# A fused retention and PReLU MLP kernel: the last two token blocks go as a pair through all eight units

## Chip, cores and metric

The kernel runs on one core of a Trainium2 chip. The metric is the device time of one execution in microseconds (us); lower is better. The engines are named as the profile names them: PE (TensorE), PEld (its weight loads), DVE (VectorE), ACT (ScalarE), POOL (GpSimd) and SP (SyncE, which issues the DMAs here).

## What is computed

```python
# retention: q, k, v are (B=8, H=8, S=576, D=64)
scores = (1 / np.sqrt(D)) * np.matmul(q, k.transpose(0, 1, 3, 2))
gamma = 1.0 - 2.0 ** (-5.0 - np.arange(H))
rel = pos[:, None] - pos[None, :]
Dmat = np.where(rel >= 0, gamma[:, None, None] ** rel[None], 0.0)
attn = np.matmul(scores * Dmat, v)
# MLP on the same tokens
x = attn.transpose(0, 2, 1, 3).reshape(4608, 512)
h = x @ w_in                                   # (4608, 2048)
g = np.maximum(h, 0) + alpha * np.minimum(h, 0)
out = g @ w_out                                # (4608, 512)
```

All of it is fp32. [...]each operand of a product is split into three pieces (a scaled high part, a low part and a difference), and each product is three matmuls.

## The kernel before, in words

**Tiling.** The 4608 tokens are 18 blocks of 256 (`kb`). The hidden width of 2048 is eight units of 256 (`u`). The work of one block on one unit is a *cell*: a first product (x pieces times w_in pieces, functions `unit` and `unit_two`), the PReLU on ACT and DVE, the split of its result into three pieces in a g tile (`split_g`: two ACT and two POOL operations), and a second product (`second`, g pieces times w_out pieces, summed in the four PSUM banks `pso`). A *visit* is one block going through several units; `order` (line 964) lists the visits. `evacuate` (L1243) takes a visit's sum out of PSUM with the help of DVE, and stores it, either as the result or, where more units are to follow, in the DRAM buffer `ok`. A later visit of the block reads it back into the tile `op`.

**Stages.** SBUF holds the split weights of four units (`wsl`, 4 x 4 tiles). So the first half of the kernel takes blocks 0 to 16 through units 0 to 3, while the attention for later blocks runs in between (`joint`, called at the cells that `todo` lists, the last at cell 56). Block 17 is the *turn*: it goes through all eight units in one visit, and behind it the weights of units 4 to 7 take the place of those of units 0 to 3. The second half takes blocks 0 to 16 through units 4 to 7.

**Singles and pairs.** `unit` (L1132) works on one block: its matmuls have 256 columns (L1151), 12 for each half of the unit, 24 for a cell. `unit_two` (L1171) works on two blocks at once: 24 matmuls for two cells, of 512 columns (L1181), with the results in `psh` for one half and in `psa` for the other. Before the change, the first half and the turn are singles, blocks 0 to 15 of the second half go in eight pairs, and block 16's second half is a single at the very end. The second product (L1232) has 512 columns in both forms.

**x pieces.** `split_x` (L1011) splits a block's x. For a single, the pieces lie in one of the two `lx` tiles (`one_room`). For a pair, `two_rooms` gives the tiles: those of unit 3's weights (`wsl[3]`) and the two `lx` tiles in turn. A block's x is kept in DRAM (`xk`) between its halves. In a pair's split DVE makes the low piece (L1057) and POOL the difference (L1061). Where two columns of pieces lie side by side, one operation takes both (512 elements); where not, each takes 256. Singles from visit `LATE_X` on use a PSUM bank of `psa` for an intermediate, which spares POOL an operation.

**Weights.** In the first half, `convert` brings the weights from the inputs' form into fp32, one quarter unit at a time, and stores those of units 4 to 7 in DRAM (`wk`); it uses the tiles `op` and `wa`. `split_w` (L750) makes three pieces of one quarter. With `raw` it reads the quarter from `wk` by DMA, and, before the change, then takes a form of its own: two ACT operations (one into `psa`) and two DVE operations that read `psa` (L765 to L774). Without `raw` it takes one ACT, one POOL (L775) and one DVE operation (L777). Unit 4's pieces go into the tiles that attention used (`planes`, L1427), and the others into `wsl[0]` to `wsl[2]`.

**What sets the order.** The code doesn't issue instructions as it is read. `do` records operations with engine, cost and dependencies, and `plan` (L226) orders them: it works out due times from the end backwards, and then fills each engine's queue forwards, the operation with the earliest due time first. PE may go at most 150 recorded operations ahead of its order in the program (`AHEAD_PE`). Big DMAs are issued no more than 30 us before they are due (`HOLD`). Operations marked `lock` (all of POOL's tensor operations and those of DVE that read two SBUF operands) are held in one order across POOL and DVE:

```python
for op in best[1]:
    ins = op.fn()
    if op.lock:
        if port and port[0] != op.eng:
            tc.add_manual_dep(ins.ins, port[1].ins.name, ..., reason="port")
        port = op.eng, ins
```

In the pair stage, `pump` (L1516) says how many second products are recorded after each half of a first product: `PUMP0` has five for the first pair and `PUMP` eight for each later one (L339), so five second products are carried from each pair into the next.

Of the kernel before, what the change touches and what calls it, by code (L numbers as in the profile page):

```python
# [17 lines left out]
ALU = mybir.AluOpType  # L18
# [3 lines left out]
def kernel(  # L22
# [10 lines left out]
    nc = tc.nc  # L33
    B, H, S, D = q.shape
    NTOK, DM = out.shape
# [3 lines left out]
    NPAIR = H // 2  # L39
# [3 lines left out]
    NCC = DM // P  # L43
    NFC = DFF // P
    NU = NFC // 2
    TB = 2 * P
    NKB = NTOK // TB
    NS = NU // 2
# [8 lines left out]
    ONE = 1.0 + 2.0 ** -12  # L57
    BELOW = 1.0 - 2.0 ** -13
# [22 lines left out]
    def piece(x):  # L81
        return x.bitcast(PIECE)
# [255 lines left out]
    LAG, HOLD_X = 2, 100.0  # L338
# [411 lines left out]
    def split_w(at, raw=None, planes=None):  # L750
        u, i = divmod(at, 4)
        if raw:
            key = (raw, "w", 0)
            dma(lambda: words_of(raw)[:, 0:DM], lambda: w32[at], P * DM * 4, [(w32m[at], 0)], [key])
        else:
            key = plain[at]
        if planes is None:
            g = Gen(wsl[u if u < NS else u - NS - 1, i])
            planes = [(g, l) for l in range(3)]
        w = w_at[u, i] = planes  # L760
        h, l, d = (lambda n=n: piece(words_of(w[n][0])[:, w[n][1] * DM:(w[n][1] + 1) * DM])
                   for n in range(3))
        hf = lambda: words_of(w[0][0])[:, w[0][1] * DM:(w[0][1] + 1) * DM]
        full = lambda: words_of(key[0])[:, key[2]:key[2] + DM]
        do("ACT", 0.64, lambda: nc.scalar.mul(h(), full(), BELOW), [key], [w[0]])  # L765
        if raw:
            hp = Gen(psa[at % 2])
            do("ACT", 0.6, lambda: nc.scalar.mul(piece(hp.get()), full(), BELOW), [key], [(hp, 0)])
            do("DVE", 0.69, lambda: nc.vector.tensor_tensor(
                out=l(), in0=full(), in1=hp.get(), op=ALU.subtract), [key, (hp, 0)], [w[1]])  # L770
            do("DVE", 0.69, lambda: nc.vector.scalar_tensor_tensor(
                out=d(), in0=hp.get(), scalar=ONE, in1=full(), op0=ALU.mult,
                op1=ALU.subtract), [key, (hp, 0)], [w[2]])
            return  # L774
        do("POOL", 1.29, lambda: nc.gpsimd.tensor_tensor(  # L775
            out=l(), in0=full(), in1=hf(), op=ALU.subtract), [key, w[0]], [w[1]], lock=True)
        do("DVE", 0.7, lambda: nc.vector.scalar_tensor_tensor(  # L777
            out=d(), in0=hf(), scalar=ONE, in1=full(), op0=ALU.mult,
            op1=ALU.subtract), [key, w[0]], [w[2]], lock=True)
# [181 lines left out]
            dma(to, lambda h2=h2: su.get()[half(h2)], (S - C) * D * 4, keys, [(vn, "s", h2)])  # L961


    order = [(kb, (0, 1, 2, 3)) for kb in range(NKB - 1)]
    order += [(NKB - 1, range(NU))]
    order += [(kb, (4, 5, 6, 7)) for kb in range(NKB - 1)]
    visits, cells, seen = [], [], {kb: 0 for kb in range(NKB)}
    for n, (kb, us) in enumerate(order):
        vis = {"kb": kb, "n": n, "has": seen[kb] > 0, "us": us}
# [28 lines left out]
        return {(l, cc): (g, (l * NCC + cc) * TB) for l in range(3) for cc in range(NCC)}, TB  # L998

    def two_rooms(n):  # L1000
        if n % 2:
            gg = [Gen(x) for x in lxs]
            return {(l, cc): (gg[cc // 2], (l * 2 + cc % 2) * DM)
                    for l in range(3) for cc in range(NCC)}, DM
        gg = [Gen(wsl[NS - 1, i]) for i in range(4)]
        at = {(2, cc): (gg[cc], 2 * DM) for cc in range(NCC)}
        at.update({(l, cc): (gg[l * 2 + cc // 2], cc % 2 * DM)
                   for l in range(2) for cc in range(NCC)})
        return at, DM
# [250 lines left out]
            P * DM * 4, [(o, 0)], [(okm[kb], m)])  # L1260


    LATE_X = next(v["n"] for v in visits if 4 in v["us"]) - 3
    spare = Gen(lxs[1])
    raws = iter([((spare, 0), kTs[1]), ((spare, 1024), qTs[1]), ((spare, 2048), was)] +
                4 * [((wsl[0, i], 0), None) for i in range(4)])
# [137 lines left out]
    assert sum(map(len, todo.values())) == len(pairs) - 2 * NPAIR  # L1404


    turn = cells.index(next(c for c in cells if c["u"] == NS)) - NS
    late = {turn - 8 + 2 * i: [16 + i] for i in range(4)}
    for i in range(3):
        for n in range(4):  # L1410
            late.setdefault(turn + 1 + i + n // 2 * LAG, []).append(20 + 4 * i + n)
    raw_rooms = [Gen(None) for _ in range(2)]
    ahead = {10 + 3 * i: 1 for i in range(16)}
    nraw = [0]

    def raw_room():
        n = nraw[0] % 3
        nraw[0] += 1
        if n == 2:
            return Gen(xs[3])  # L1420
        g = Gen(None)
        was = raw_rooms[n] if raw_rooms[n].ops else vnm[n]
        g.before, g.tile = list(was.ops), vns[n]
        raw_rooms[n] = g
        return g

    def planes():  # L1427
        for x in (kxs, qxs, kns[0], kns[1], kTs[0], kTs[1], qTs[0], qTs[1]):
            yield Gen(x), 0
        g = Gen(ats)  # L1430
        yield g, 0
        yield g, 1
        for x in (sus, was):
            yield Gen(x), 0

    def start_x(vis):
        kb = vis["kb"]
        if "from" not in vis and (kb not in xb or NPAIR * (ready_kb[kb] + 1) in done):
            fetch_x(vis)

    pend = []
    turned_to = next(v["n"] for v in visits if 4 in v["us"])
    two = [(visits[n], visits[n + 1]) for n in range(turned_to + 1, len(visits) - 1, 2)]
    for i, (va, vb) in enumerate(two):
        va["two"], vb["two"] = (i, 0), (i, 1)
    visits[-1]["two"] = len(two), 0
    homes_two = {}

    def next_x(vis):
        start_x(vis)  # L1450
        if "from" in vis and "x" not in vis:
            if "two" not in vis:
                split_x(vis)
            else:
                i, side = vis["two"]
                if not side:
                    homes_two[i] = two_rooms(i)
                split_x(vis, homes_two[i], side)

    def at_cell(cell):  # L1460
        n, vis = cell["n"], cell["vis"]
        next_x(vis)
        for _ in range(ahead.get(n, 0)):
            convert((op_, 0), was, None)
        for at in late.get(n, ()):
            if at == 16:
                planes_of.append(planes())
            split_w(at, raw_room(), [next(planes_of[0]) for _ in range(3)] if at < 20 else None)
        unit(cell)
        pend.append(cell)  # L1470
        if len(pend) > LAG:
            second(pend.pop(0))
        split_g(cell)
        for x in todo.get(n, ()):
            joint_(x)

    planes_of = []
    of = {}
    for cell in cells:
        of.setdefault(cell["vis"]["n"], []).append(cell)  # L1480
    for cell in cells[8:]:
        vis = cell["vis"]
        if vis["n"] > turned_to:
            break
        at_cell(cell)
        nxt = vis["n"] + 1
        if vis["n"] < turned_to:
            if cell["last"] or vis["n"] > 3:
                start_x(visits[nxt])
                if cell["last"]:  # L1490
                    next_x(visits[nxt])
        elif cell["u"] in (NS + 1, NS + 2):
            next_x(visits[nxt + cell["u"] - NS - 1])

    ga_rooms = [xs[2], xs[3], xs[4]]
    ga_kept = [raw_rooms[n] for n in range(2)]
    nga = [0]

    def ga_room():
        n = nga[0] % 5  # L1500
        nga[0] += 1
        if n < 3:
            return Gen(ga_rooms[n])
        g = Gen(None)
        g.before, g.tile = list(ga_kept[n - 3].ops), vns[n - 3]
        ga_kept[n - 3] = g
        return g

    queue = list(pend)
# [1 line left out]
    def ahead_g(k=2):  # L1511
        for c in queue[:k]:
            if "ga" in c and "g" not in c:
                split_g(c)

    def pump(k):  # L1516
        for _ in range(k):
            if queue and "ga" in queue[0]:
                ahead_g(1)
                second(queue.pop(0))  # L1520
                ahead_g()

    for i, (va, vb) in enumerate(two):
        ca, cb = of[va["n"]], of[vb["n"]]
        queue += ca + cb
        for nu, (a, b) in enumerate(zip(ca, cb)):
            ga = ga_room()
            for f in range(2):
                unit_two(va, vb, a["u"], ga, f)
                if f:  # L1530
                    for side, c in enumerate((a, b)):
                        c["ga"] = ga, lambda ga=ga, side=side: words_of(ga)[
                            :, 0:2 * DM].rearrange("p (f s t) -> p f s t", f=2, s=2)[:, :, side]
                    ahead_g()
                pump((PUMP if i else PUMP0)[nu][f])
            nxt = va["n"] + 2 + (nu - 1)
            if nu in (1, 2) and nxt < len(visits):
                next_x(visits[nxt])
    for cell in of[visits[-1]["n"]]:
        unit(cell)  # L1540
        queue.append(cell)
        pump(3)
        ahead_g()
    pump(len(queue))
    best = plan()

# [40 lines left out]
```

## Time and profile before

| what | value |
|---|---|
| median of 3 runs | 931.44 us (930.61 to 931.87) |
| the profiled execution's own time | 930.41 us |
| its span, first to last instruction | 928.7 us |
| cells as singles / in pairs | 80 / 64 |
| DMA issues that matter here: `xk<-x`, `x<-xk` | 18, 17 of 512 KB |
| `ok<-o`, `op<-ok` | 34 of 256 KB, 17 of 512 KB |
| `vn<-wk`, `x<-wk` (weights of units 4 to 7) | 11 and 5 of 256 KB |

The page of the profile gives each engine's busy time, then groups of instructions by line, engine and operation as "out<-in", with their count, busy time and mean. The chain of work that ended last is followed back from the last instruction: at each step to what released it. A view by stages gives each engine's busy time in chosen stretches, the instructions begun there, PE's granted clock, the DMA engines' share, and GB/s. L1151 is line 1151 of the kernel.

### The profile page before, as it was taken

Reading aid. Unit: us, or ns where it says so; the run is one execution under the profiler, and the core shown is the slowest. Engines: PE = TensorE matmul, PEld = TensorE weight load, DVE = VectorE, ACT = ScalarE, POOL = GpSimd, SP = SyncE. Lnnn points to the kernel's source line nnn. Section 1 sums busy time; section 2 is a strip of 40 time slices with the busy share of each in tenths; the row PEclk is TensorE's granted clock in tenths of the full one; section 3 lists DMA queues with packets and bytes.
Section 4 is the critical chain, followed back from the end, with each engine's and each line's share of the span. In section 5 each row is a group of like instructions: output and inputs, shape, how many; then the busy total and the mean of one; then the engine's idle time right before and its main releaser. Section 6 shows DMA issues by size and latency. Waiting matters only on the chain.

```text
span 928.7 us, 20968 instructions
## 1 busy us (share of the span) xinstructions
PE 918.4 (99%) x8101; PEld 779.4 (84%) x8101; DVE 532.5 (57%) x1070; ACT 552.6 (60%) x1178; POOL 579.3 (62%) x491
## 2 busy tenths in 40 slices
PE   8999999999999999999999999999999999999998
PEld 7676798988888898988999988888888888888887
DVE  7677666667666667766755764443454444434333
ACT  4566557566666667666876885554546363635342
POOL 5676867558765677655666465837465655647363
PEclk9999999999999999999999999999999999999999
DMA  9997587798887859864444421121212222221112
GB/s 231 241 233 144 127 203 151 176 206 175 195 199 193 193 138 221 191 150 130 148 137 147 126 80 68 47 91 46 91 54 82 68 86 95 70 68 46 46 46 68
DMA packets 235524, 120.93 MB, mean 130 GB/s; under 512 B 203408, under 2 KB 203424, under 8 KB 235424
## 3 DMA queue, kind: packets, MB, share of 16 engines
q1 hardware_dynamic: 235424, 119.59, 50.9%
q8 instruction: 64, 1.05, 0.5%
q14 instruction: 36, 0.29, 0.1%
HBM read 74.19 MB, written 31.98 MB: 114 GB/s over the span
## 4 chain that ended last, share of the span: by engine, by line
PE 90%; DMA 3%; DVE 2%; POOL 2%; SPq 1%; issue 1%; ACT 1%; POOLq 0%; DVEq 0%; ACTq 0%
PE pso L1232 39%; PE psh L1151 22%; PE psh L1181 9%; PE psa L1181 9%; PE psh L851 3%; PE psa L913 2%; PE psh L1082 2%; PE pso L1113 1%; SPq L208 1%; POOL w L775 1%; DMA kn<-in_k_dram 1%; DMA w<-in_moe_w_in_dram 1%; PE psh L903 1%; PE psa L910 1%; DMA lx<-in_moe_w_in_dram 0%
## 5 line engine op out<-in xcount | busy, mean ns | idle before, releaser
L1232 PE MATMUL pso<-w,g 128*128 128x512 f32 x1416 | 347.1, 392 | 0.0
L1232 PEld LDWEIGHTS pso<-w,g 128*128 128x128 f32 x1416 | 259.6, 188 | 50.7
L1151 PEld LDWEIGHTS psh<-lx,w 128*128 128x128 f32 x1608 | 202.4, 191 | 8.4 <-ACT x L870 1.1
L1151 PE MATMUL psh<-lx,w 128*128 128x256 f32 x1608 | 208.5, 284 | 0.7 <-ACT x L870 0.5
L1211 POOL TENSOR_TENSOR g<-g 128x512 fp32r<-128x512 f32 x136 | 176.0, 1294 | 24.2 <-DVE w L1057 4.1
L1208 POOL TENSOR_TENSOR g<-ga,g 128x512 fp32r<-128x512 f32 x72 | 93.2, 1294 | 122.9 <-ACT g L1204 107.9
L1159 DVE SCALAR_TENSOR_TENSOR ga<-psh,ga 128x256 f32<-128x256 f32 x144 | 60.6, 421 | 70.6 <-ACT ga L1158 68.9
L1158 ACT COPY ga<-psh 128x256 f32<-128x256 f32 x144 | 53.5, 372 | 69.5 <-PE psh L1151 60.8
L1208 POOL TENSOR_TENSOR g<-x,g 128x512 fp32r<-128x512 f32 x40 | 51.7, 1295 | 63.5 <-ACT g L1204 61.0
L1165 DVE SCALAR_TENSOR_TENSOR ga<-psh,malpha,ga 128x256 f32<-128x256 f32 x144 | 68.6, 477 | 22.4 <-ACT psh L1162 21.4
L1061 POOL TENSOR_TENSOR lx<-lx 128x512 fp32r<-128x512 f32 x48 | 61.9, 1296 | 20.1 <-DVE lx L1057 13.1
L1162 ACT ACTIVATE psh<-ga 128x256 f32<-128x256 f32 x144 | 55.7, 387 | 30.4 <-DVE ga L1159 30.2
L1204 ACT ACTIVATE g<-ga 128x512 fp32r<-128x512 f32 x72 | 45.4, 631 | 22.3 <-DVE ga L1165 15.0
L1208 POOL TENSOR_TENSOR g<-vn,g 128x512 fp32r<-128x512 f32 x24 | 31.1, 1294 | 41.6 <-ACT g L1204 38.4
L931 DVE SCALAR_TENSOR_TENSOR at<-psa,pf,mask 64x512 f32<-64x512 f32 x48 | 36.0, 750 | 25.8 <-PE psa L910 24.9
L1206 ACT ACTIVATE g<-ga 128x512 fp32r<-128x512 f32 x72 | 44.7, 621 | 0.0
L1250 DVE TENSOR_TENSOR op<-pso,op 128x512 f32<-128x512 f32 x34 | 23.3, 686 | 36.8 <-PE pso L1232 36.7
L1204 ACT ACTIVATE g<-x 128x512 fp32r<-128x512 f32 x40 | 25.1, 630 | 32.1 <-PE pso L1232 17.1
L1188 DVE SCALAR_TENSOR_TENSOR x<-psh,x 128x512 f32<-128x512 f32 x20 | 13.8, 690 | 45.0 <-PE psh L1181 45.0
L851 PEld LDWEIGHTS psh<-at,vn 128*64 128x64 f32 x864 | 27.7, 137 | 10.8 <-issue 6.0
L1057 POOL TENSOR_TENSOR lx<-x,lx 128x512 fp32r<-128x512 f32 x24 | 31.1, 1295 | 8.7 <-ACT lx L1054 5.4
L1181 PE MATMUL psh<-lx,w 128*128 128x512 f32 x144 | 34.7, 389 | 0.0
(292 smaller groups left out, 1695.9 us busy)
## 6 DMA issues: line engine op xcount, KB each, us to landing
xk<-x SPq DMA_DIRECT2D x18, 512.0 KB, 4.1
out_dram<-o SPq DMA_DIRECT2D x36, 256.0 KB, 2.0
ok<-o SPq DMA_DIRECT2D x34, 256.0 KB, 3.2
x<-xk SPq DMA_DIRECT2D x17, 512.0 KB, 5.7
op<-ok SPq DMA_DIRECT2D x17, 512.0 KB, 4.0
qx<-in_q_dram SPq DMA_DIRECT2D x96, 72.0 KB, 3.4
kx<-in_k_dram SPq DMA_DIRECT2D x96, 72.0 KB, 3.1
kn<-in_k_dram SPq DMA_DIRECT2D x48, 144.0 KB, 3.7
```

What stands on the lines that cost most here:

```text
L851: nc.tensor.matmul(pv[i].get()[half(h2), (j - js[0]) * C:(j - js[0] + 1) * C], vns[n % 2][:, h2, j], mt.get()[:, h2, j], start=True, stop= ...
L1061: lambda l=l, d=d, h=view(0, c): nc.gpsimd.tensor_tensor(out=piece(d()), in0=h(), in1=l(), op=ALU.subtract),
L1151: nc.tensor.matmul(at(b), w[:, c0:c0 + P], xp(l, cc), start=(n == 0 and cc == 0), stop=(n > 0 and cc == NCC - 1), skip_group_check=True)
L1158: do("ACT", 0.36, lambda g=g, at=at: nc.scalar.copy(g(), at(1)), [(ph, 1)], [(ga, f)])
L1159: do("DVE", 0.42, lambda g=g, at=at: nc.vector.scalar_tensor_tensor(out=g(), in0=at(0), scalar=ONE, in1=g(), op0=ALU.mult, op1=ALU.subtrac ...
L1162: do("ACT", 0.39, lambda g=g, at=at: nc.scalar.activation(at(1), g(), ACTF.Relu, scale=-1.0), [(ga, f)], [(ph, 1)])
L1165: do("DVE", 0.48, lambda g=g, at=at, fc=fc: nc.vector.scalar_tensor_tensor(out=g(), in0=at(1), scalar=malpha[:, fc:fc + 1], in1=g(), op0=A ...
L1181: nc.tensor.matmul(p.get(), w[:, c0:c0 + P], piece(words_of(g)[:, o:o + DM]), start=(l != 1 and cc == 0), stop=(l > 0 and cc == NCC - 1))
L1204: do("ACT", 0.64, lambda: nc.scalar.mul(piece(to.get()[:, 2]), whole(), BELOW), both, [(to, 2)])
L1208: do("POOL", 1.29, lambda: nc.gpsimd.tensor_tensor(out=piece(to.get()[:, 1]), in0=whole(), in1=to.get()[:, 2], op=ALU.subtract), both + [( ...
L1211: do("POOL", 1.29, lambda: nc.gpsimd.tensor_tensor(out=piece(to.get()[:, 2]), in0=to.get()[:, 0], in1=to.get()[:, 1], op=ALU.subtract), [( ...
L1232: nc.tensor.matmul(a[2 * m + b].get(), piece(g.get()[:, l, f, m * P:(m + 1) * P]), w_piece(u, 2 + f, l), start=(cell["first"] and f == 0 a ...
```

## The change

The visits are ordered anew. Blocks 0 to 15 go through units 0 to 3 as singles. Then blocks 16 and 17 go as a pair through units 3, 0, 1, 2 and as a pair through units 4 to 7, on the same x pieces. Then blocks 0 to 15 go in eight pairs through units 4 to 7. Every cell from the turn on is in a pair: 64 cells as singles and 80 in pairs. Block 17's half sum is now stored and read back like that of every other block.

The x pieces of the first pair, and of every second pair after it, lie in the tiles that attention used (`planes`); the pairs between use `wsl[3]` as before. Unit 4's weight pieces go into the two `lx` tiles. The weights of unit 5 + u are split in two steps, by the new `split_later`: those of its first product after unit u's first product in the first pair, and those of its second product after unit u's second product for block 17. The raw quarters are read into `x3`, `x4` and the two `ga` tiles. The form of `split_w` with two DVE operations on `psa` is gone: all quarters take the one with an ACT, a POOL and a DVE operation, the last two under the lock. `LATE_X` is 15 in place of 14.

```diff
@@ split_w @@
         do("ACT", 0.64, lambda: nc.scalar.mul(h(), full(), BELOW), [key], [w[0]])
-        if raw:
-            hp = Gen(psa[at % 2])
-            do("ACT", 0.6, lambda: nc.scalar.mul(piece(hp.get()), full(), BELOW), [key], [(hp, 0)])
-            do("DVE", 0.69, lambda: nc.vector.tensor_tensor(
-                out=l(), in0=full(), in1=hp.get(), op=ALU.subtract), [key, (hp, 0)], [w[1]])
-            do("DVE", 0.69, lambda: nc.vector.scalar_tensor_tensor(
-                out=d(), in0=hp.get(), scalar=ONE, in1=full(), op0=ALU.mult,
-                op1=ALU.subtract), [key, (hp, 0)], [w[2]])
-            return
         do("POOL", 1.29, lambda: nc.gpsimd.tensor_tensor(
@@ order of the visits @@
-    order = [(kb, (0, 1, 2, 3)) for kb in range(NKB - 1)]
-    order += [(NKB - 1, range(NU))]
-    order += [(kb, (4, 5, 6, 7)) for kb in range(NKB - 1)]
+    order = [(kb, (0, 1, 2, 3)) for kb in range(NKB - 2)]
+    order += [(kb, (3, 0, 1, 2)) for kb in (NKB - 2, NKB - 1)]
+    order += [(kb, (4, 5, 6, 7)) for kb in (NKB - 2, NKB - 1, *range(NKB - 2))]
@@ two_rooms @@
-        if n % 2:
-            gg = [Gen(x) for x in lxs]
-            return {(l, cc): (gg[cc // 2], (l * 2 + cc % 2) * DM)
-                    for l in range(3) for cc in range(NCC)}, DM
+        if n % 2 or n == 0:
+            rooms_of = ((g, i * DM) for g, i in planes())
+            return {(l, cc): next(rooms_of) for l in range(3) for cc in range(NCC)}, DM
@@
-    LATE_X = next(v["n"] for v in visits if 4 in v["us"]) - 3
+    LATE_X = NKB - 3
@@ when weights are split @@
-    turn = cells.index(next(c for c in cells if c["u"] == NS)) - NS
-    late = {turn - 8 + 2 * i: [16 + i] for i in range(4)}
-    for i in range(3):
-        for n in range(4):
-            late.setdefault(turn + 1 + i + n // 2 * LAG, []).append(20 + 4 * i + n)
+    turn = cells.index(of[NKB - 2][0])
+    late = {turn - 4: [16], turn - 3: [17]}
...
@@ start_x @@
-        if "from" not in vis and (kb not in xb or NPAIR * (ready_kb[kb] + 1) in done):
+        if vis.get("two", (0,))[0] == 1:
+            at, step, side = visits[vis["n"] - 2]["x"]
+            vis["x"] = at, step, side
+        elif "from" not in vis and (kb not in xb or NPAIR * (ready_kb[kb] + 1) in done):
             fetch_x(vis)
@@ pairs @@
-    turned_to = next(v["n"] for v in visits if 4 in v["us"])
-    two = [(visits[n], visits[n + 1]) for n in range(turned_to + 1, len(visits) - 1, 2)]
+    singles = NKB - 2
+    two = [(visits[n], visits[n + 1]) for n in range(singles, len(visits), 2)]
     for i, (va, vb) in enumerate(two):
         va["two"], vb["two"] = (i, 0), (i, 1)
-    visits[-1]["two"] = len(two), 0
...
+    def split_first(at):
+        if at % 2 == 0:
+            planes_of[:] = [Gen(lxs[at // 2 % 2])]
+        split_w(at, Gen(xs[3 + at % 2] if at < 18 else gas[at % 2]), [(planes_of[0], at % 2 * 3 + l) for l in range(3)])
...
@@ the cells of the singles @@
-        elif cell["u"] in (NS + 1, NS + 2):
-            next_x(visits[nxt + cell["u"] - NS - 1])
+        if nxt == singles:
+            if cell["u"] < 2:
+                next_x(visits[nxt + cell["u"]])
...
@@ pump @@
-                second(queue.pop(0))
+                c = queue.pop(0)
+                second(c)
+                if c["vis"]["n"] == singles + 1 and c["u"] < NS - 1:
+                    split_later(c["u"], 1)
                 ahead_g()
+
+    def split_later(u, half_of):
+        for n in range(2):
+            at = (NS + 1 + u) * 4 + 2 * half_of + n
+            split_w(at, Gen(gas[at % 2]))
@@ the pairs @@
                 pump((PUMP if i else PUMP0)[nu][f])
+            if i == 0:
+                if a["u"] < NS - 1:
+                    split_later(a["u"], 0)
+                else:
+                    split_first(18)
+                    split_first(19)
...
-    for cell in of[visits[-1]["n"]]:
-        unit(cell)
-        queue.append(cell)
-        pump(3)
-        ahead_g()
     pump(len(queue))
```

The rest of the diff is room keeping: `raw_room` and its counters go, and the pairs' `ga` tiles begin with `vn0` and `vn1` in place of `x2`.

More of the change, by code (lines that the diff above doesn't have):

```diff
@@ L1404 @@
     assert sum(map(len, todo.values())) == len(pairs) - 2 * NPAIR
-    turn = cells.index(next(c for c in cells if c["u"] == NS)) - NS
-    late = {turn - 8 + 2 * i: [16 + i] for i in range(4)}
-    for i in range(3):
-        for n in range(4):
-            late.setdefault(turn + 1 + i + n // 2 * LAG, []).append(20 + 4 * i + n)
+    of = {}
+    for cell in cells:
+        of.setdefault(cell["vis"]["n"], []).append(cell)
+    turn = cells.index(of[NKB - 2][0])
+    late = {turn - 4: [16], turn - 3: [17]}
     raw_rooms = [Gen(None) for _ in range(2)]
     ahead = {10 + 3 * i: 1 for i in range(16)}
[L1414 to L1425, printed above, removed]
     def planes():
@@ L1465, in at_cell @@
         for at in late.get(n, ()):
-            if at == 16:
-                planes_of.append(planes())
-            split_w(at, raw_room(), [next(planes_of[0]) for _ in range(3)] if at < 20 else None)
+            split_first(at)
         unit(cell)
@@ L1477 @@
     planes_of = []
-    of = {}
-    for cell in cells:
-        of.setdefault(cell["vis"]["n"], []).append(cell)
+    def split_first(at):
+        if at % 2 == 0:
+            planes_of[:] = [Gen(lxs[at // 2 % 2])]
+        split_w(at, Gen(xs[3 + at % 2] if at < 18 else gas[at % 2]), [(planes_of[0], at % 2 * 3 + l) for l in range(3)])
     for cell in cells[8:]:
         vis = cell["vis"]
-        if vis["n"] > turned_to:
+        if vis["n"] == singles:
             break
@@ L1486 @@
         nxt = vis["n"] + 1
[L1487 to L1491, printed above, removed]
-        elif cell["u"] in (NS + 1, NS + 2):
-            next_x(visits[nxt + cell["u"] - NS - 1])
+        if nxt == singles:
+            if cell["u"] < 2:
+                next_x(visits[nxt + cell["u"]])
+        elif cell["last"] or vis["n"] > 3:
+            start_x(visits[nxt])
+            if cell["last"]:
+                next_x(visits[nxt])
     ga_rooms = [xs[2], xs[3], xs[4]]
-    ga_kept = [raw_rooms[n] for n in range(2)]
-    nga = [0]
+    nga = [3]
     def ga_room():
@@ L1504, in ga_room @@
         g = Gen(None)
-        g.before, g.tile = list(ga_kept[n - 3].ops), vns[n - 3]
-        ga_kept[n - 3] = g
+        g.before, g.tile = list(raw_rooms[n - 3].ops or vnm[n - 3].ops), vns[n - 3]
+        raw_rooms[n - 3] = g
         return g
```

## The prediction, made before the changed kernel ran

> **What bounds the kernel now.** First the head and the busy totals of the page.
>
> ```profile
> span 928.7 us, 20968 instructions
> PE 918.4 (99%) x8101; PEld 779.4 (84%) x8101; DVE 532.5 (57%) x1070; ACT 552.6 (60%) x1178; POOL 579.3 (62%) x491
> ```
>
> PE is never idle for long; the other engines have a third of the time free. So the question is what PE does in each stage. The chain of work that ended last, asked for the stretches around the turn (start, length, piece):
>
> ```profile
> 497.73 2.87 PE psh L1151 x24
> 500.61 2.75 PE pso L1232 x12
> 503.35 2.87 PE psh L1151 x24
> ...
> 572.84 2.72 PE psh L1181 x12
> 575.56 2.72 PE psa L1181 x12
> 578.28 5.44 PE pso L1232 x24
> ...
> ```
>
> From about 440 us the chain is PE alone, back to back. A cell of a single block costs 2.87 + 2.75 = 5.62 us. Two cells of a pair cost 2.72 + 2.72 for the first product and 5.44 for the second: 10.88, or 5.44 a cell. Over whole pairs (L1181 on psh begins a pair at 653.24 and the next at 696.84) it is 43.60 for eight cells, 5.45 each. The end of the same chain:
>
> ```profile
> 912.59 2.87 PE psh L1151 x24
> 915.46 9.56 PE pso L1232 x42
> 925.02 0.05 issue
> 925.07 0.69 DVE o L1255
> ```
>
> The last single cell's chain through ACT, DVE and POOL is fully covered: 42 matmuls were held back for it. From 925.07 on there are the last evacuation and its store, 3.6 us to the span's end.
>
> Then the reserve of the others, by stage (columns: PE, PEld, DVE, ACT, POOL busy):
>
> ```profile
> 200.00:250.00 50.00, 49.88 (x587) 43.83 (x586) 34.17 (x77) 35.53 (x84) 39.72 (x32) 1.00 0.92 199
> 440.00:481.00 41.00, 41.00 (x291) 37.27 (x286) 26.31 (x53) 33.45 (x76) 28.94 (x23) 1.00 0.41 131
> 548.00:584.00 36.00, 36.00 (x160) 29.82 (x159) 16.87 (x26) 23.16 (x44) 21.46 (x18) 1.00 0.13 45
> 610.00:653.60 43.60, 43.60 (x194) 35.95 (x193) 18.74 (x28) 22.63 (x41) 25.59 (x21) 1.00 0.23 73
> ```
>
> POOL and the DVE operations marked lock are put in one order by the code (lines 1547 to 1555), so their times add. I call the sum the **port**. In 200 to 250 it was 39.72 + 4.6 (three weight conversions at 0.42 + 0.42 + 0.69 us of DVE) = 44.3 of 50 us, 89%, and PE still ran 49.88. In a steady pair it is 25.59 + 2.77 = 28.4 of 43.6.
>
> **What the Trainium skill says.** "TensorE: Matmul & The Clock Gate", section "Wait — 56ns, not 53.3ns?": a warm matmul starts every N/2.4 GHz plus 2.5 ns. The trace has 2.72/12 = 226.7 ns for 512 columns and 2.87/24 = 119.6 for 256: the difference, 107.1 ns for 256 columns, agrees with 2.4 GHz, but the fixed part is 12.5 ns here. The measurement decides; this fixed part is what a pair saves. "SBUF — State Buffer", section "Who interferes with whom": a DVE instruction with two SBUF inputs blocks against a GpSimd one that reads SBUF, one with a single SBUF input does not. The code's lock follows that: the old weight split reads its second operand from PSUM and takes no lock, the new one does. The trace shows the waits of the ordering (below), not the hardware's. "Perfetto Trace Analysis", section "Identifying the Most-Contended Engine": matmul busy time is a poor measure; so I use start-to-start times, not the 99%.
>
> **The change part by part.**
>
> *Pairs for singles.* 16 cells (eight of block 17, four of block 16's first half, four of its second) leave the single form for eight pair cells. First product: 8 x (2 x 2.87 - 5.44) = 2.40 us less. Second: 16 x (2.75 - 2.72) = 0.48 less. Sum -2.88, all of it on PE, which sets the end.
>
> *One more trip through DRAM.* Block 17 was summed over eight units in PSUM; now its half sum is stored and read back: 36 evacuated visits for 35, two more stores of 256 KB, one more read of 512 KB (3.2 and 4.0 us to landing). A pair's surplus over 16 x 2.72 is 43.60 - 43.52 = 0.08 for its two evacuations, so one more is 0.04; with rounding +0.1 on PE. The copy on ACT (0.59) and the DVE operations (0.69 each) lie under PE. Against it, block 16's x is read back and split once less (one DMA and about eight POOL and DVE operations); block 17 had no second split. SP issues at 0.3 to 0.6 us each with DMA at 0.13 to 0.23 of its time there: nothing.
>
> *The tail.* The last five second products now follow the last pair's first product with no other work between. From the end of such a first product to its last piece the steady trace has about 5.7 us (psa unit ends near 615.1, POOL L1211 ends at 620.8). Two second products (5.44) can be held back for it, three if g's three buffers allow. Between 0 and 0.5; I take +0.2. After that POOL needs 2.59 a cell against PE's 2.72. Evacuation and store stay 3.6.
>
> *Attention must be finished for both blocks at the turn.* Block 17's x was needed at 480.9, now both are, but what they wait for, the last attention copy (L870), starts at 441.1. That leaves 40 us, in which the pieces go into attention's tiles. One of these (wa) is also the conversions' buffer, so the last conversion, which ended at about 492, must come some 20 us earlier; the planner's due times pull it. Port in that stage: 28.94 + about 5 of DVE locks, + 4 x (0.74 + 0.42) x 2 for two narrow splits, + 2 x 1.97 for two weights, less a late split (2.6) and a conversion or two: about 42 of 41 us on paper if nothing moved, but work of 10 us can go into 400 to 440, where POOL is below 0.7 busy. Nothing taken, up to 2 us if it doesn't fit.
>
> *The weights of units 4 to 7.* Sixteen splits change form: ACT 0.63 + 0.59 and DVE 2 x 0.68, unlocked, become ACT 0.63, POOL 1.28 and DVE 0.69, both in the port: +1.97 each, +31.5 us of port. The moved DMA reads (16 of 256 KB, about 3 us to landing) stay on SP, later than before. Two lie before the turn; two, and the six first-product ones, in the first pair (but units 7's two only as it ends); six second-product ones in the second pair.
>
> The second pair is the tightest place. The narrow x split there, by form (count, busy, mean ns, idle before and releaser):
>
> ```profile
> L1057 DVE TENSOR_TENSOR w<-x,w 128x256 fp32r<-128x256 f32 x28 | 10.9, 421 | 22.3 <-POOL g L1208 14.4 <-POOL g L1211 4.6 <-POOL w L1061 3.2
> L1061 POOL TENSOR_TENSOR w<-w,w 128x256 fp32r<-128x256 f32 x28 | 20.1, 743 | 11.6 <-DVE w L1057 11.6
> ```
>
> g: 8 x 2.59 = 20.7. Weights: 6 x 1.97 = 11.8, and 3.9 left over from unit 7. x for the third pair: 8 x (0.42 + 0.74) = 9.3. Handing over: POOL to DVE 0.03, DVE to POOL about 0.11 (637.50 to 637.53, 638.22 to 638.30, 636.05 to 636.20), 16 turns x 0.14 = 2.2. Sum 47.9, against 43.6 of PE. But three g can be made ahead in the first pair (-7.8): 40.1, 92%. The first pair then has 8 x 2.59 + 6 x 1.97 + 0.8 = 33.3 of 35.4, 94%. It fits, above the 89% that was seen to cost nothing. I take +0.1; the bounds are 0 and 6.
>
> DVE waits at these locks with the chains of L1188 and L1193 queued behind, and those release the next g; POOL has g itself behind it. That is the danger.
>
> **Sum.** -2.88 + 0.1 + 0.2 + 0.1 = -2.5. The profiled execution took 930.41 (span 928.68 and 1.73 around it): 927.9. The median 931.44 lies 1.0 above that execution, so **928.9**.
>
> **The rivals.** Faster or slower than 931.44 by over 0.2% (1.9 us) is about what can be told from no change: 929.6 and 933.3.
>
> *Gain eaten.* The spare 5% of the port isn't usable: the x pieces can't begin before unit 3's last second product frees its tiles, some 11 us into the second pair, and from there to its end x 9.3 + weights 11.8 + four g 10.4 + turns 2.0 = 33.5 stand against 32.7. With 0.8 over, and as much in the first pair: 930.5, no difference. For it: L1057 stood 22.3 us waiting on POOL even in quiet pairs. Against it: PE may put second products later, and a pair later the port has 12 us free.
>
> *Slower: the port in the second pair.* A locked DVE operation stands behind an unlocked one of 0.69 to 0.75, on average half of it, 0.36, while POOL waits its turn: L1061's 11.6 us over 28 shows 0.41 each already. With the handover 0.5 a turn; 14 turns x 0.5 = 7 on 42.0 makes 49 against 43.6: +5.4 us of PE idle, 934.3. It decides from 4.4 us of overflow on.
>
> *It doesn't do what it says.* The planner keeps singles' speed, say by splitting the pair's x late at the turn, so that PE waits 2 to 3 us once: 931.5.
>
> **How the numbers follow.** Forecast 928.9 (928.2 to 929.6): 0.58. Gain eaten 0.20 and the late turn 0.08: together 0.28 within 0.2%. Slower 0.14. The range reaches from 928.0, the full 2.9 with the scatter of 0.5 that the runs show, to 932.5, which leaves out the slower case and little else.
>
> **What would show it.** PE busy about 916; no L1151 after the turn; the first pair begins near 481, and each later one takes 43.6. Waits of PE for g (POOL L1211) or x (L1061) between 490 and 565 would be the port; a gap near 481 the late turn; a gap before the last second products the tail. The forecast is wrong if PE's idle time after 440 is over 1 us besides the end, or if a pair form's cell isn't 5.45 in the new pairs.

## The result and the profile after

The changed kernel took 929.44 us (median of 22 runs, 927.5 to 933.23) against 931.87 for the kernel before in the same runs: ratio 0.9977, 95% interval 0.9969 to 0.9985. A second set gave 928.82 against 931.96, ratio 0.9967 (0.9957 to 0.9976). So it is faster by 2 to 3 us; 928.9 was forecast, 2.5 us below.

The profiled execution took 931.02 (span 929.3), in the slower half of the 22. It has to be read by stages and not by its span. The head of its page:

```profile
span 929.3 us, 20609 instructions
PE 915.8 (99%) x7909; PEld 770.7 (83%) x7909; DVE 518.9 (56%) x1040; ACT 542.0 (58%) x1164; POOL 601.2 (65%) x525
```

There are 192 matmuls fewer and as many weight loads fewer; PE is busy 2.6 us less, POOL 21.9 us more. In the changed kernel L1151 is now L1141, L1181 is L1171, L1232 is L1222. L1198 and L1201 are POOL's two operations for a g tile, L766 and L768 POOL's and DVE's for a weight quarter, L1051 and L1047 those for an x split. The chain of work that ended last, from the last singles on (start, length, piece):

```profile
471.71 2.87 PE psh L1141 x24
474.59 2.29 PE pso L1222 x10
476.88 2.87 PE psh L1141 x24
479.75 4.11 PE pso L1222 x18
483.86 2.72 PE psh L1171 x12
486.58 2.72 PE pso L1222 x12
489.30 2.72 PE psa L1171 x12
...
513.78 2.73 PE pso L1222 x12
516.60 0.64 ACT g L1194
517.31 1.31 POOL g L1198
518.64 0.70 DVE w L768
519.48 1.30 POOL g L1198
520.77 0.77 issue
521.58 1.30 POOL g L1201
522.92 2.12 PE pso L1222 x8
525.04 2.72 PE psa L1171 x12
```

The turn comes at 483.7, and no 256-column matmul follows it. The x for the two blocks was there in time. In the second pair the chain leaves PE for once: a second product waits for its g, which POOL could begin only after a weight split of DVE (L768) that came first in the common order. This is the port (POOL and the locked DVE operations taken together), and what it costs is small: from start to start, two matmuls there take 0.24 and 0.11 us more than their 0.227. It is the only place after the turn where one takes over 0.1 us more.

The end of the chain:

```profile
901.05 2.72 PE psa L1171 x12
903.77 21.77 PE pso L1222 x96
925.54 0.04 issue
925.58 0.69 DVE o L1245
```

Eight second products were held back for the tail, where I had thought of two or three, and they run without a gap.

The stages of the changed kernel (columns: PE, PEld, DVE, ACT, POOL busy), the second pair last:

```profile
440.00:481.00 41.00, 40.96 (x289) 36.76 (x288) 22.74 (x50) 30.99 (x76) 32.26 (x29) 1.00 0.32 108
481.00:517.00 36.00, 36.00 (x160) 29.82 (x159) 17.08 (x26) 20.83 (x39) 20.69 (x17) 1.00 0.40 127
517.00:560.50 43.50, 43.42 (x192) 35.62 (x191) 22.41 (x38) 29.12 (x59) 32.98 (x29) 1.00 0.31 98
```

I cut the profiled executions, two of each kernel, at the first matmul of the first split cell, at the turn (the 57th such cell before the change, the first pair after it: 64 cells are then begun in both, and equally many second products are done) and at the start of the last matmul:

| stage, us | before | before, second | changed | changed, second |
|---|---|---|---|---|
| head, to the first split cell | 101.31 | 102.16 | 103.72 | 101.84 |
| from there to the turn | 379.40 | 380.39 | 379.98 | 378.62 |
| turn to the last matmul | 443.91 | 443.93 | 441.44 | 441.31 |
| from there to the end | 4.06 | 4.06 | 4.18 | 4.18 |

The stage that the change is about repeats to 0.1 us and is 2.5 us shorter. The head moves by 2.4 us in these four executions, with SP's queue in the same order in both kernels there; that is the main reason why the first profile of the changed kernel has a longer span than that of before.

### The profile page after: what moved, and what is told of

Read it like the earlier page. It is cut to its first block, busy times and chain, and to the rows that moved or that the text cites. A ratio compares the mean times of both kernels' runs of the same rounds, so it can differ in the third digit from the quotient of the medians.

```text
span 929.3 us, 20609 instructions
## 1 busy us (share of the span) xinstructions
PE 915.8 (99%) x7909; PEld 770.7 (83%) x7909; DVE 518.9 (56%) x1040; ACT 542.0 (58%) x1164; POOL 601.2 (65%) x525
## 4 chain that ended last, share of the span: by engine, by line
PE 86%; DMA 5%; POOL 3%; SPq 2%; issue 1%; DVE 1%; ACT 1%; POOLq 0%; ACTq 0%; DVEq 0%
PE pso L1222 38%; PE psh L1141 16%; PE psa L1171 12%; PE psh L1171 11%; PE psh L842 3%; SPq L208 2%; PE psa L904 2%; DMA vn<-su 1%; DMA w<-in_q_dram 1%; POOL w L766 1%; PE psh L1072 1%; DMA w<-in_moe_w_in_dram 1%; DMA w<-in_v_dram 1%; PE pso L1103 1%; DMA w<-in_moe_w_out_dram 1%
## 5 line engine op out<-in xcount | busy, mean ns | idle before, releaser
L1222 PE MATMUL pso<-w,g 128*128 128x512 f32 x1416 | 343.8, 391 | 0.1
L1222 PEld LDWEIGHTS pso<-w,g 128*128 128x128 f32 x1416 | 261.2, 188 | 52.3 <-POOL g L1201 0.5
L1201 POOL TENSOR_TENSOR g<-g 128x512 fp32r<-128x512 f32 x136 | 175.6, 1293 | 25.7 <-DVE kT L1047 3.9
L1141 PE MATMUL psh<-lx,w 128*128 128x256 f32 x1344 | 174.4, 285 | 0.6 <-ACT x L861 0.6
L1141 PEld LDWEIGHTS psh<-lx,w 128*128 128x128 f32 x1344 | 168.4, 191 | 6.2 <-ACT x L861 0.7
L1198 POOL TENSOR_TENSOR g<-ga,g 128x512 fp32r<-128x512 f32 x56 | 72.3, 1291 | 76.4 <-ACT g L1194 46.2
L1198 POOL TENSOR_TENSOR g<-x,g 128x512 fp32r<-128x512 f32 x48 | 62.1, 1294 | 75.7 <-ACT g L1194 69.2
L1198 POOL TENSOR_TENSOR g<-vn,g 128x512 fp32r<-128x512 f32 x32 | 41.4, 1295 | 46.3 <-ACT g L1194 38.6
L1149 DVE SCALAR_TENSOR_TENSOR ga<-psh,ga 128x256 f32<-128x256 f32 x112 | 47.1, 420 | 35.1 <-ACT ga L1148 33.0
L1155 DVE SCALAR_TENSOR_TENSOR ga<-psh,malpha,ga 128x256 f32<-128x256 f32 x112 | 53.3, 477 | 14.4 <-ACT psh L1152 13.9
L1152 ACT ACTIVATE psh<-ga 128x256 f32<-128x256 f32 x112 | 43.3, 387 | 22.3 <-DVE ga L1149 21.5
L1222 PE MATMUL pso<-lx,g 128*128 128x512 f32 x216 | 53.7, 391 | 0.0
L1194 ACT ACTIVATE g<-x 128x512 fp32r<-128x512 f32 x48 | 30.2, 630 | 40.1 <-PE pso L1222 23.3
L1194 ACT ACTIVATE g<-ga 128x512 fp32r<-128x512 f32 x56 | 35.4, 631 | 22.7 <-DVE ga L1155 18.0
L1222 PEld LDWEIGHTS pso<-lx,g 128*128 128x128 f32 x216 | 40.0, 188 | 9.4 <-ACT psa L1181 1.4
L1047 POOL TENSOR_TENSOR lx<-x,lx 128x512 fp32r<-128x512 f32 x26 | 33.6, 1293 | 12.5 <-ACT lx L1044 8.4
L1051 POOL TENSOR_TENSOR lx<-lx 128x512 fp32r<-128x512 f32 x28 | 36.1, 1292 | 5.0 <-DVE w L768 2.1
```

What stands on the lines that cost most here:

```text
L1051: lambda l=l, d=d, h=view(0, c): nc.gpsimd.tensor_tensor(out=piece(d()), in0=h(), in1=l(), op=ALU.subtract),
L1141: nc.tensor.matmul(at(b), w[:, c0:c0 + P], xp(l, cc), start=(n == 0 and cc == 0), stop=(n > 0 and cc == NCC - 1), skip_group_check=True)
L1149: do("DVE", 0.42, lambda g=g, at=at: nc.vector.scalar_tensor_tensor(out=g(), in0=at(0), scalar=ONE, in1=g(), op0=ALU.mult, op1=ALU.subtrac ...
L1152: do("ACT", 0.39, lambda g=g, at=at: nc.scalar.activation(at(1), g(), ACTF.Relu, scale=-1.0), [(ga, f)], [(ph, 1)])
L1155: do("DVE", 0.48, lambda g=g, at=at, fc=fc: nc.vector.scalar_tensor_tensor(out=g(), in0=at(1), scalar=malpha[:, fc:fc + 1], in1=g(), op0=A ...
L1194: do("ACT", 0.64, lambda: nc.scalar.mul(piece(to.get()[:, 2]), whole(), BELOW), both, [(to, 2)])
```

## The experiments

Ratios are to the kernel before, with 95% intervals. "Stage" is the time from the turn to the start of the last matmul in the profiled execution, 441.3 to 441.4 in the changed kernel. In kernels with lines put in, the line numbers shift by a few: in experiments 3, 5 and 6 L1225 is the second product, in 3 L1172 is a pair's first product, and in 5 L1201 is the first of POOL's two operations for g.

**1. The changed kernel again.**

> The changed kernel, unaltered. Theory (16 cells cheaper on PE, nothing else): ratio to the kernel before 0.9972 to 0.9978, a turn and pair stage (from the first pair's first matmul to the last matmul) of 441.7 us as in its first profile, while the time before the first split cell moves by up to 2.5 us from run to run, since the queues are the same there. Rival (the change costs something in the attention stage): the first pair begins at least 2 us later than 481 in every profile, this one too.

Measured: ratio 0.9967 (0.9957 to 0.9976), stage 441.31, turn at 480.46. The stage is that of the first profile, 441.44 as the table counts it. The late turn of the first profile (483.7) did not come back: of the 3.2 us, 1.9 lie in the head and 1.4 between the first split cell and the turn. The ratio lies a little below what I expected of it, with an interval that takes most of it in.

**2. The kernel before again.**

> The kernel before, for a second profile. Theory (the head scatters, the attention stage is not slowed by the change): the first split cell begins between 101 and 104 us, and from there to the first matmul of the first pair 447.0 us as in its first profile, within 0.3. Rival: the attention stage itself scatters by 1 us or more, and the profiles of one run each can't be told apart there.

Measured: ratio to the other runs 1.0006 (0.9994 to 1.0018). The first split cell begins at 102.16, and from there to the first pair it is 447.87, 1.0 us more than in the first profile (446.88). The two profiles of the changed kernel differ by 1.4 us in the attention stage. So it scatters by 1 us or more, and the rival holds for it: a cost of under 1 us there can't be read from single profiles.

**3. The first product of the pairs in halves.** It takes away the saving of the 512-column form and leaves all else.

```diff
-                    nc.tensor.matmul(p.get(), w[:, c0:c0 + P], piece(words_of(g)[:, o:o + DM]), ...)
+                    for h in range(2):
+                        nc.tensor.matmul(p.get()[:, h * TB:(h + 1) * TB], w[:, c0:c0 + P],
+                                         piece(words_of(g)[:, o + h * TB:o + (h + 1) * TB]), ...)
```

> All ten pairs keep their order and tiles, but each 512-column matmul of the first product is done as two of 256: 960 more matmuls. Theory (a matmul has a fixed part of 12.5 ns, and this is what a pair saves): +12.0 us on the changed kernel, 119.6 ns from start to start. Rival (a single's cell is dearer by its second product too, since each change between 256 and 512 columns costs): +12.0 and 0.03 for each of 80 cells, +14.4.

Measured: 940.97, ratio 1.0101 (1.0086 to 1.0116), 12.2 us above the changed kernel of the same set (928.82). Stage 454.63, 13.3 more. The chain of this kernel in a quiet pair:

```profile
712.66 2.87 PE psh L1172 x24
715.53 2.75 PE pso L1225 x12
718.28 2.87 PE psa L1172 x24
721.15 4.16 PE pso L1225 x18
```

The first product is at 2.87 again and a second product that follows it at 2.75, as in a single's cell. Both parts of the saving are the form's. But a second product that follows another second product costs no 0.03, so the stage grows by 13.3, between the two expectations.

**4. Without the splits of the late weights.** Units 4 to 7 use pieces of units 0 to 2, so the DMA reads and the ACT, POOL and DVE operations of 16 quarters are left out.

```diff
         u, i = divmod(at, 4)
+        if u >= NS:
+            w_at[u, i] = w_at[(u - NS) % 3, i]
+            return
```

> Leaves out the splits of the weights of units 4 to 7 and their DMA reads (the second half uses pieces of other units, so its results are others). It takes 31.5 us of work from POOL and DVE's locked operations around the turn. Theory (that work lies under PE): within 0.5 us of the changed kernel, ratio to before 0.9970 to 0.9978. Rival (gain eaten by the port): 1.0 to 2.5 us faster than the changed kernel, ratio 0.995 to 0.9965.

Measured: 928.68, ratio 0.9969 (0.9959 to 0.9978), against 0.9967 for the changed kernel in the same set. Stage 441.09, no gap between matmuls. So 31.5 us of work in the port cost 0.2 to 0.35 us of time, and the rival "gain eaten" falls.

**5. The POOL operation of the late splits done twice.**

```diff
         do("POOL", 1.29, lambda: nc.gpsimd.tensor_tensor(
             out=l(), in0=full(), in1=hf(), op=ALU.subtract), [key, w[0]], [w[1]], lock=True)
+        if raw:
+            do("POOL", 1.29, lambda: nc.gpsimd.tensor_tensor(
+                out=l(), in0=full(), in1=hf(), op=ALU.subtract), [key, w[0]], [w[1]], lock=True)
```

> The POOL operation of each of the sixteen splits of the weights of units 4 to 7 is done twice: 20.5 us more of POOL around the turn, 6 of them in the first pair and 8 in the second. Theory (the port is 92 to 94% full there by my sum): it overflows by 5.6 us in the first pair and 6.7 in the second, less what can move: 4 to 12 us slower than the changed kernel, PE idle between 490 and 565. Rival (second products can be put off and the port has room): under 1.5 us.

Measured: 943.45, ratio 1.0124 (1.011 to 1.0138), 14.6 us above the changed kernel. Stage 456.58, of which 1.4 are six matmuls that the other kernels do before the turn. PE's longest wait (line, releaser: us in total, times, longest):

```profile
PE pso L1225 <- POOL g L1201: 9.3, 1, 9.3
```

The mechanism is the expected one, but it costs more than the upper end. From matmul to matmul PE's waits for g in the trace make 12.1 us beyond 0.227 each, all of them late in the second pair. Behind the longest the granted clock is a half from 564.9 to 575.1 us, and the matmuls there take 2.1 us more. The waits alone would be about the upper end; the clock, which the expectation did not have, took it beyond.

**6. Only in the second pair.** As in 5, for the six quarters of the second products of units 5 to 7 (`if u > NS and i > 1`).

> The POOL operation is done twice for six of the sixteen weight quarters alone, those of the second products of units 5 to 7, which fall into the second pair: 6 x 1.29 = 7.7 us more of POOL there. Theory (the second pair has 3.5 us of port left by the prediction's sum): the pair stage grows by about 4 us, at most 5. Rival (the room of the later pairs can be used too): under 1 us.

Measured: 941.08, ratio 1.0109 (1.0085 to 1.0132); stage 453.12, 11.7 more for 7.7 us of work. Both expectations fail: the second pair had no port to spare. The stages of this kernel around the gap (columns: PE, PEld, DVE, ACT, POOL busy, granted clock):

```profile
540.00:554.00 14.00, 14.00 (x63) 11.37 (x61) 8.02 (x12) 8.83 (x19) 11.20 (x9) 1.00 0.49 165
554.00:558.50 4.50, 0.38 (x3) 0.03 (x1) 2.11 (x4) 2.95 (x9) 2.69 (x4) 0.83 0.00 0
558.50:564.00 5.50, 4.94 (x11) 3.58 (x12) 2.10 (x6) 1.98 (x7) 3.29 (x4) 0.52 0.00 0
564.00:568.00 4.00, 1.56 (x5) 0.71 (x5) 0.00 (x0) 1.15 (x2) 3.92 (x6) 0.90 0.00 0
568.00:571.50 3.50, 3.50 (x11) 2.77 (x10) 0.00 (x0) 0.00 (x0) 3.42 (x6) 0.62 0.00 0
571.50:576.00 4.50, 4.50 (x21) 3.72 (x20) 1.32 (x3) 1.74 (x3) 4.42 (x4) 1.00 0.00 0
```

PE stands for want of g (4.3, 1.1, 1.8 and 1.1 us from matmul to matmul beyond 0.227, 8.4 in all with a 0.1), which is the added work. Then the granted clock falls to about a half, and 512 columns start every 0.43 us: 3.5 us more. The two make 11.9.

**7. The first pair through units 0, 1, 2, 3.** Unit 3's tiles, which the third pair's x needs, then come free later.

```diff
-    order += [(kb, (3, 0, 1, 2)) for kb in (NKB - 2, NKB - 1)]
+    order += [(kb, (0, 1, 2, 3)) for kb in (NKB - 2, NKB - 1)]
...
-            nxt = va["n"] + 2 + (nu - 1)
-            if nu in (1, 2) and nxt < len(visits):
+            x_at = 2 if i == 1 else 1
+            nxt = va["n"] + 2 + (nu - x_at)
+            if nu in (x_at, x_at + 1) and nxt < len(visits):
```

> The first pair goes through units 0, 1, 2, 3 in place of 3, 0, 1, 2, and the split of x for the third pair is recorded one unit later. Unit 3's tiles, which the third pair's x needs, come free about 13.6 us later, 19 us before that pair begins. Theory (port nearly full): x 9.3 us, weights 3.9 to 7.9, two g 5.2 and the turns 1.5 make 20 to 24 us against 19: 1 to 5 us slower than the changed kernel, PE waiting for x at the third pair. Rival (the planner finds room): within 0.7 us of it.

Measured: 932.13, ratio 1.0004 (0.9994 to 1.0014); the changed kernel had 0.9967 and 0.9977. Stage 444.27, 2.9 more. PE's matmuls at the beginning of the third pair, with idle time and releaser in brackets:

```profile
563.35 2.10 PE L1171 MATMUL psh<-w,lx 128*128 128x512 f32 x7
566.55 1.42 PE L1171 MATMUL psh<-w,lx 128*128 128x512 f32 x5 [1.09 <-POOL w L1051]
569.14 3.01 PE L1222 MATMUL pso<-w,g 128*128 128x512 f32 x12 [1.17 <-POOL g L1201]
```

The first pair's odd order of units is worth the whole gain of the change. Without it PE waits for x and then for the g that stood behind it.

**8. DVE's late operations out of the common order.** They keep their data dependencies.

```diff
-            op1=ALU.subtract), [key, w[0]], [w[2]], lock=True)
+            op1=ALU.subtract), [key, w[0]], [w[2]], lock=not raw)
...
-                        keys + key(2, c), key(1, c), lock=True)
+                        keys + key(2, c), key(1, c), lock=rooms is None)
```

> The DVE operations of the late weight splits and of the pairs' x splits keep their data dependencies but leave the common order with POOL, so that DVE and POOL may read SBUF at once. Theory (the order costs nothing as long as nobody on PE waits): pair stage 441.4 us within 0.4, the two engines' operations longer where they overlap. Rival (the order hides a loss): faster than the changed kernel by 1 us or more.

Measured: 928.86, ratio 0.9972 (0.9959 to 0.9985). Stage 442.15, 0.8 more than the changed kernel's second profile, a bit over the expected 0.4. The split of the late weights on DVE from 460 to 570 us, in the changed kernel's second profile (count, busy, mean ns, idle before and releaser):

```profile
L768 DVE SCALAR_TENSOR_TENSOR w<-w,ga 128x512 fp32r<-128x512 f32 x12 | 8.1, 690 | 10.9 <-POOL g L1198 7.3 <-POOL w L766 2.8 <-POOL g L1201 0.8
```

and without the order:

```profile
L768 DVE SCALAR_TENSOR_TENSOR w<-w,ga 128x512 fp32r<-128x512 f32 x12 | 16.8, 1414 | 2.5 <-ACT w L765 2.5
```

The same operation takes twice as long, so the wait is now inside it. Taking the order away gains nothing: the rival falls.

**9. Without the conversions too.** As 4, and the 16 conversions of the late weights in the first half are left out (`ahead = {}`).

> Leaves out the conversions of the weights of units 4 to 7 in the first half as well as their splits (the second half uses other units' pieces). 16 conversions are 45 us of POOL and DVE's locked operations and 8 MB of DMA in the attention stage. Theory (attention stage bound by PE): 0.5 to 1.5 us faster than the changed kernel, mostly the DMA waits of PE at the attention products. Rival (the earlier conversions cost the attention stage 2 us or more): 2.5 to 4 us faster.

Measured: 925.90, ratio 0.9949 (0.9933 to 0.9965). Against the changed kernel's two ratios that is 1.7 to 2.6 us less: more than the theory had, and only its upper end reaches the rival's range. From the first split cell to the turn it has 377.76 us against 379.98 and 378.62. In the changed kernel PE waits there for the state DMAs of the attention (us in total, times, longest; the first profile, then the second):

```profile
PE psh L842 <- DMA vn<-su: 1.9, 3, 1.4
PE psh L842 <- DMA vn<-su: 1.4, 3, 0.6
```

This wait stands in all eight profiles of kernels that have both the new order and the conversions, with 1.1 to 2.8 us. It is not in this run, and in neither profile of the kernel before, which has the conversions too, but some of them later. So the change does make PE wait in the attention stage. Yet the stage is no longer for it: 380.1 us in the mean of those eight profiles, 379.9 in the two of the kernel before. What became shorter in its place is not shown.

## Why the prediction was right, step by step

**PE sets the end; 16 cells in pairs save 2.88 us.** Right. The stage is 2.5 us shorter, and experiment 3 gives the 256-column form back and with it 2.87 and 2.75. The fixed part of a matmul, 12.5 ns against the 2.5 that the Trainium skill has in "TensorE: Matmul & The Clock Gate", section "Wait — 56ns, not 53.3ns?", is what is saved: 960 more matmuls would be 12.0 us. Experiment 3 gave 12.2 in the medians and 13.3 in the stage, which also has the changes from 256 to 512 columns in it.

**One more trip through DRAM, +0.1; the tail, +0.2.** 36 stores and 18 reads, as counted. After the last matmul there are 4.18 in place of 4.06 us. In the tail no matmul is late, so its 0.2 wasn't spent: the planner held back eight second products where I allowed two or three. The extra evacuation can't be told from nothing.

**Attention must be finished for both blocks.** Right in that nothing was late at the turn: the chain goes from L1222 to L1171 without a gap. Wrong in size: POOL's part of the last conversion began at 454.6 in place of 490.1 us, 36 us earlier, not 20. POOL had room for it. But the stage was put at "nothing taken", and PE now waits 1.1 to 2.8 us in it for the state DMAs (experiment 9). That the time to the turn is nevertheless the same (378.6 to 380.0 against 379.4 to 380.4) was luck: no term of the prediction says why.

**The port in the second pair.** The place and the sign were right and the cost was 0.35 us where 0.1 was taken. The sum was not. I had 33.3 us of 35.4 in the first pair, with three g made ahead there, which left the second with 40.1 of 43.6. These are the two in the changed kernel's second profile (columns as in the stages above):

```profile
481.00:516.00 35.00, 35.00 (x156) 29.00 (x155) 16.64 (x25) 21.36 (x39) 19.25 (x15) 1.00 0.41 128
516.00:560.00 44.00, 43.93 (x194) 36.02 (x194) 22.12 (x38) 28.85 (x60) 33.93 (x31) 1.00 0.29 96
```

The ordered DVE operations add 4.16 us in the first (L768), and 4.84 and 3.71 in the second (L768 and L1047). So the port has 23.4 of 35.0 us and 42.5 of 44.0, before any handing over. The first pair made four g, not eight, and the second its full eight: none was made ahead. So the second pair is full, as experiment 6 shows from the other side: 7.7 us more made PE stand for 8.4. The view that I gave to the rival, by release times and deadlines (33.5 us of work against 32.7), was nearer to it there: it was 0.8 over where 0.35 was lost. But it had as much for the first pair, where nothing was lost. The forecast was saved not by the 5% of room that it claimed, but because the work just fits, and only with unit 3 first: experiment 7 loses 2.9 us. That it fits is luck as far as the sum goes.

**The slower rival, half a DVE operation at each turn of the port.** It didn't come, and its reading was wrong. L1061's 11.6 us were not 0.41 for each of 28 operations, but seven waits in the trace, four of 2.4 and three of 0.68, and each has the 0.42 of the DVE operation itself in it. In the changed kernel's second profile, from 513 to 560 us, POOL handed the turn to DVE nine times, where sixteen were counted, and each time the DVE operation began 0.03 us later: none stood behind an unlocked one.

**The sum.** -2.88 + 0.35 for the port and +0.12 behind the last matmul is -2.4; measured by stages, -2.5 + 0.12 = -2.4; forecast, -2.5. The range held. What the forecast did not name is the scatter: the head moves by over 2 us, nearly as much as the gain.

**What stays open.** Why the head scatters. Also what makes up, in the attention stage, for PE's new waits there.

## What to carry to other kernels

When PE is busy all the time, a fixed cost for each matmul is worth money: widening 16 cells from 256 to 512 columns gave 0.15 us for every 12 matmuls saved. What pays for it is room and other engines' time. Where two engines are held in one order, sum their work between the moment when its inputs come free and the moment when its result is due, and not over a whole stage. Here the sum over the second pair had 8% to spare and the one between release and deadline had none, and the trace shows the pair full. A short span says little when the start scatters: cut two profiles at the same instructions, and compare the stages.

## What was not expected of the hardware

A stall of PE can cost more than its length. In experiment 6, after waits of 4.3 and 1.1 us, matmuls of 512 columns started every 0.43 us for some 4 us (granted clock 0.52 in that window), and again after 1.8 and 1.1 us: 8.4 us of waiting became 11.9. The Trainium skill describes this clock in "TensorE: Matmul & The Clock Gate", section "What's actually happening": half rate after an idle window of about 3.4 us. The traces agree on the half rate, with 0.43 against 0.227 us, but the second time no single wait was as long as that. In experiment 7 two waits of 1.4 and 1.3 us left the clock full.

In experiment 8, a DVE operation with two SBUF operands grew from 690 to 1414 ns beside POOL, while POOL's split of the same weights (L766) grew from 1296 to 1369. This agrees with the exclusive lock in "SBUF — State Buffer", section "Who interferes with whom", and here DVE bore most of it.
